# Weights converted 1024 columns at a time at fixed places in the program, and every engine's order fixed from the start

## The chip, the core and the metric

The kernel runs on one core of one Trainium2 chip. The time is the device time of one execution in microseconds (us). Before the change, three executions took 1067.61, 1067.10 and 1067.68 us, a median of 1067.61. The core has five engines that run side by side, each through its own queue of instructions in order: PE (matrix products; its weight loads are listed as PEld), DVE (vector), ACT (activation functions, scaled copies), POOL (elementwise work) and SP (starts DMA transfers). Results of PE land in PSUM, everything else is in SBUF.

## The reference

Eight batches of windowed attention (8 heads, 576 rows, head size 64, window 128, a linear bias per head) make a matrix x of 4608 rows by 512 columns. A two-layer network follows:

```python
attn = softmax(q @ k.T / 8 + bias, window of 128) @ v        # 8 batches x 8 heads x 576 x 64
x = attn laid out as (4608, 512)
h = x @ w_in                                                 # 512 -> 2048
g = h * tanh(log(1 + exp(h)))                                # mish
out = g @ w_out                                              # 2048 -> 512
```

q, k and v are 32-bit floats. [...]

## The kernel before

**Products.** Each 32-bit operand of the network is held as two parts, an upper part rounded to the format PE reads quickly, and the lower part that is left. A product is three matmuls: upper by upper, upper by lower, lower by upper.

**Weights.** There are 16 tiles, eight of `w_in` (raw `wi`, finished `si`) and eight of `w_out` (raw `wo`, finished `so`), called wi0 to wi7 and wo0 to wo7 here. A raw tile holds 1024 numbers of 64 bits per partition, read as pairs of 32-bit words (low, high). `convert_w` (lines 141 to 179) makes a 32-bit float of each and splits it, in two halves of 512 columns. For a half, ACT makes a scaled copy `t` (tile `ti` or `to`) and DVE shifts it by three bits and joins 29 bits of the low word into it. The sign then comes back in one of two ways: ACT takes the sign beforehand and POOL multiplies by it (`signs`), or DVE joins the sign bit with a third instruction. Last ACT writes the upper part and POOL subtracts it from the value, which gives the lower part.

**Chunks.** The 4608 rows go in nine chunks of 512. The first eight are rows 0 to 511 of each batch, the ninth collects the 64 left-over rows of all eight. `attention(b)` (line 401) makes chunk b's x in four pairs of heads, each of two units (`unit`: scores on PE, reduces and exps, a `fold` on POOL, a scale, transposes on PE, a mask on DVE, `values` on PE, `split_x`) and a small unit for the left-over rows. `first(c, j)` (line 433), j from 0 to 7, multiplies x by one `si` tile (24 matmuls into `h`) and ACT applies mish (`g`). `second(c, half, j, t)` (line 484) multiplies g by `so` tile j in 6 matmuls into `po`, in 32 steps: 16 for the first 256 rows, two for each j, then 16 for the rest. `parts` (line 452) splits g for it: ACT copies (`gh`), POOL subtracts (`gl`). The stages are attention(0), first of chunk 0, second of chunk 0 with attention(1) laid between its steps, first of chunk 1, and so on.

**Order.** SP's instructions keep the order in which they are written. Those of the other four engines are placed by a scheduler until the end of `first` of chunk 1, where `fixed` is set (line 534); from there they keep the written order too. `convert_next` (line 513) takes the next weight off a list: at three times inside attention(0) with both halves signed by ACT and POOL, in `first` of chunk 0 (none signed), and in `second` of chunk 0 (one half signed). The 16th weight, wo7, is loaded late into two smaller tiles, since space only then comes free.

Of the kernel before, what the change touches and what calls it, by code (L numbers as in the profile page):

```python
# [8 lines left out]
F32 = mybir.dt.float32  # L9
F32R = mybir.dt.float32r  # L10
U32 = mybir.dt.uint32
BF16 = mybir.dt.bfloat16
AF = mybir.ActivationFunctionType
ALU = mybir.AluOpType

WINDOW = 128
P = 128


class InOrder:  # L20


    def __init__(self, tc, engine, fixed):
        self.tc, self.engine, self.fixed = tc, engine, fixed

    def __getattr__(self, name):
        method = getattr(self.engine, name)

        def call(*args, **kwargs):
            ins = method(*args, **kwargs)  # L30
            if self.fixed:
                self.tc.keep_in_program_order(ins)
            elif name == "activation" and args[2] in (AF.Exp, AF.Mish, AF.Sign):

                self.tc.stamp_issue_order_token(ins.ins, "act_table")
            return ins

        return call

# [2 lines left out]
def attention_mish_mlp(  # L42
# [17 lines left out]
    nc = tc.nc  # L60
# [3 lines left out]
    CH = 512  # L64
# [26 lines left out]
    for t in vb:  # L91
# [5 lines left out]
    make_upper_triangular(nc, masks[:, 1, :])  # L97
    xs = dram.tile([NCC, P, CH], F32, tag="xs", name="xs")

    pe, dve, act, pool, sp = engines = [  # L100
        InOrder(tc, e, e in (nc.sync,))
        for e in (nc.tensor, nc.vector, nc.scalar, nc.gpsimd, nc.sync)
    ]

    bits = w_in.dtype != F32
    raw_w, split = {}, {}
# [32 lines left out]
    def convert_w(kind, j, signs):  # L141

        halves = raw_w.pop((kind, j))
        w = split[(kind, j)] = big(f"s{kind}{j}", F32R)
        for a, raw in enumerate(halves):
            if bits:
                low, high = raw[:, 0::2], raw[:, 1::2]  # L150
                val = high.bitcast(F32)
                t = ff.tile([P, 512], F32, tag="gh", name=f"t{kind}{j}_{a}", bufs=3)
                tb = t.bitcast(U32)

                act.activation(t, val, AF.Copy, scale=2.0**-112)
                if a < signs:
                    act.activation(val, val, AF.Sign)
                    out_ = tb
                else:
                    out_ = high  # L160
                dve.tensor_scalar(
                    out=out_, in0=tb, scalar1=3, scalar2=None, op0=ALU.logical_shift_left
                )
                dve.scalar_tensor_tensor(
                    out=out_, in0=low, scalar=29, in1=out_, op0=ALU.logical_shift_right,
                    op1=ALU.bitwise_or,
                )
                if a < signs:
# [6 lines left out]
            else:  # L175
                val = raw[:, :512].bitcast(F32)
            up, low = (w[:, 1024 * a + k : 1024 * a + k + 512] for k in (0, 512))
            act.activation(up, val, AF.Copy)
            pool.tensor_tensor(out=low, in0=val, in1=up.bitcast(F32), op=ALU.subtract)
# [10 lines left out]
    xt = {}  # L190
# [46 lines left out]
    def unit(b, p, half):  # L237
# [43 lines left out]
        def fold():  # L281
            sm, pz = st["sm"], st["pz"]
            two = pz if half else pz[:, 1:4:2]
            pool.tensor_tensor(out=two[:, :, :P], in0=two[:, :, :P], in1=two[:, :, P:], op=ALU.add)
            dve.tensor_scalar(out=sm, in0=sm, scalar1=1e-9, scalar2=None, op0=ALU.add)
            dve.reciprocal(sm, sm)

        def scale():
# [51 lines left out]
    def last_unit(b, p):  # L340
# [24 lines left out]

        def fold():
            sm, pz = st["sm"], st["pz"]
            dve.tensor_scalar(out=sm, in0=sm, scalar1=1e-9, scalar2=None, op0=ALU.add)
# [64 lines left out]
    def first(c, j):
        h = ps.tile([P, 2, CH], F32, tag="s", name=f"h{c}_{j}", bufs=2)
        for t in range(2):
            k = 0
            for cc in range(NCC):
                x = xt[(c, cc)]
                for w_, x_ in ((0, 0), (0, 1), (1, 0)):
                    k += 1  # L440
                    pe.matmul(
                        h[:, t, :], lhsT=w_part("i", j, w_, cc)[:, t * P : (t + 1) * P],
                        rhs=x[:, x_, :], start=(k == 1), stop=(k == 3 * NCC),
                    )
# [3 lines left out]
        act.activation(gt[(c, j // 2)][:, f : f + 2, :], h, AF.Mish)  # L448
# [61 lines left out]
    for w in conv[:-1]:  # L510
        load_w(*w)

    def convert_next(signs):
        if conv and conv[0] in raw_w:
            convert_w(*conv.pop(0), signs)

    early = [(k, lambda: convert_next(2)) for k in (3.6, 5.6, 7.6)]
    for _, work in sorted(attention(0) + early, key=lambda s: s[0]):
        work()

    for c in range(B + 1):
        for j in range(NJ):
            if c == 0:
                while ("i", j) not in split:
                    convert_next(0)
            if j == NJ - 1:
                parts(c, 0, 0)
                parts(c, 0, 1)
            first(c, j)
            if c == 0:  # L530
                convert_next(0)
# [84 lines left out]
```

## Time and profile before

| what | us |
|---|---|
| median of three executions | 1067.61 |
| the profiled execution | 1068.16 |
| its span, first instruction to last | 1066.4 |
| PE busy in the span | 1004.8 |
| first 90.9 us: PE busy | 44.83 of 84.20 |
| 133.9 to 218.6 (second of chunk 0): PE busy | 74.03 of 84.70 |

The profiled execution is 1.76 us longer than its span and 0.55 us longer than the median. All work records at line 30, where the helper `InOrder` issues it, so groups go by the names of tiles. In a row such as `so<-wo,so 128x512 fp32r<-128x512 f32 x2` the output stands left of the arrow, the inputs right of it, then shapes and types, and x2 says that two like instructions are drawn together. A bracket at a row's end is the idle time before it and the instruction that ended it. [...]

### The profile page before, as it was taken

How to read it: one execution, taken by the hardware profiler on the slowest of the kernel's cores; microseconds unless marked ns; L12 is line 12 of the kernel's file. 1: busy time of each engine (PE TensorE's matmuls, PEld its weight loads, DVE VectorE, ACT ScalarE, POOL GpSimd, SP SyncE). 2: the span in 40 equal slices, each digit the busy share in tenths (PEclk: the TensorE clock that was granted, in tenths of full speed). 3: DMA queues.
4: the chain of work that ended last, by engine and by line, in shares of the span. 5: the costliest groups of instructions: out<-in, count | busy, mean ns of one | idle time of the engine just before them, and what ended most of it. 6: DMA issues, size and time to landing. Idle time of an engine off the chain costs nothing.

```text
span 1066.4 us, 14184 instructions
## 1 busy us (share of the span) xinstructions
PE 1004.8 (94%) x5280; PEld 787.6 (74%) x5280; DVE 417.3 (39%) x1155; ACT 390.1 (37%) x937; POOL 324.0 (30%) x281
## 2 busy tenths in 40 slices
PE   4657987999999999999999999999999999999998
PEld 2335855788778877787778777877788778888886
DVE  3788189610671066305640375026601670010000
ACT  2445466422451254215431453244323442231121
POOL 3453667400431034104320343024301440151042
PEclk9568997999999999999999999999999999999999
DMA  8940021300221012200320031001200201010001
GB/s 272 399 150 11 1 65 37 90 33 1 60 84 41 1 51 67 67 1 26 92 67 1 25 92 58 10 24 59 72 31 1 61 33 41 1 41 20 1 1 40
DMA packets 52133, 59.32 MB, mean 56 GB/s; under 512 B 13024, under 2 KB 32608, under 8 KB 52064
## 3 DMA queue, kind: packets, MB, share of 16 engines
q1 hardware_dynamic: 50880, 57.69, 16.9%
q8 instruction: 42, 0.69, 0.3%
q10 hardware_dynamic: 1184, 0.72, 0.2%
q14 instruction: 27, 0.22, 0.1%
HBM read 47.91 MB, written 10.49 MB: 55 GB/s over the span
## 4 chain that ended last, share of the span: by engine, by line
PE 87%; DVE 6%; issue 3%; DMA 2%; ACT 1%; SPq 1%; POOL 0%; DVEq 0%; POOLq 0%
PE h L30 37%; PE po L30 36%; PE s L30 8%; PE o L30 5%; DVE pz L30 2%; DVE wo L30 1%; SPq L30 1%; DMA wi<-in_moe_w_in_dram 1%; DVE wi L30 1%; DVE sm L30 1%; DMA nb<-in_relb_dram 1%; DMA first<-in_k_dram 0%; DVE to L30 0%; DVE ti L30 0%; DMA qd<-in_q_dram 0%
## 5 line engine op out<-in xcount | busy, mean ns | idle before, releaser
L30 PE MATMUL h<-x,si 128*128 128x512 f32 x1728 | 396.5, 391 | 0.0
L30 POOL TENSOR_TENSOR gl<-g,gh 128x512 fp32r<-128x512 f32 x144 | 189.9, 1322 | 637.0 <-ACT gh L30 552.2
L30 PEld LDWEIGHTS h<-x,si 128*128 128x128 f32 x1728 | 326.0, 189 | 68.7 <-issue 0.8
L30 PE MATMUL po<-so,gh 128*128 128x512 f32 x1152 | 326.4, 403 | 2.8 <-POOL so L30 1.6
L30 PEld LDWEIGHTS po<-so,gh 128*128 128x128 f32 x1152 | 207.1, 189 | 53.4 <-ACT x L30 6.9
L30 DVE CUSTOM_DVE_ANT_0 pz<-s,nb 128x256 f32<-128x256 f32 (+1 forms) x256 | 84.5, 386 | 321.0 <-PE s L30 321.0
L30 PE MATMUL po<-so,gl 128*128 128x512 f32 x576 | 179.5, 393 | 0.0
L30 ACT ACTIVATE pz<-pz,mx 128x256 f32<-128x256 f32 (+1 forms) x256 | 120.3, 471 | 149.8 <-DVE mx L30 149.7
L30 ACT ACTIVATE g<-h 128x1024 f32<-128x1024 f32 x72 | 74.0, 1028 | 275.1 <-PE h L30 275.1
L30 PEld LDWEIGHTS po<-so,gl 128*128 128x128 f32 x576 | 108.4, 188 | 23.7
L30 ACT ACTIVATE gh<-g 128x512 fp32r<-128x512 f32 x144 | 88.4, 620 | 51.4 <-PE po L30 49.8
L30 DVE TENSOR_TENSOR pz<-s,masks 128x1024 f32<-128x1024 f32 x64 | 78.2, 1222 | 23.4 <-PE s L30 23.4
L30 POOL TENSOR_TENSOR pz<-pz 128x256 f32<-128x256 f32 x64 | 65.4, 1022 | 48.9 <-ACT pz L30 45.6
L30 DVE TENSOR_TENSOR pz<-pz,sm 128x512 f32<-128x512 f32 x56 | 53.8, 960 | 48.3 <-POOL pz L30 48.0
L30 DVE COPY ob<-po 128x512 f32<-128x512 f32 x18 | 12.4, 690 | 118.0 <-PE po L30 118.0
L30 PE MATMUL s<-qk 64*128 64x128 f32 (+1 forms) x448 | 58.4, 379 | 0.0
L30 PE MATMUL o<-pz,va 128*64 128x128 f32 (+1 forms) x560 | 56.4, 332 | 2.0 <-DVE pz L30 2.0
L30 PEld LDWEIGHTS o<-pz,va 128*64 128x64 f32 x560 | 34.1, 139 | 30.7 <-issue 12.3
L30 ACT ACTIVATE x<-o 128x512 fp32r<-128x512 f32 x32 | 19.1, 597 | 88.6 <-PE o L30 88.6
L30 PE MATMUL s<-ident,pz 128*128 128x128 f32 x256 | 41.4, 287 | 8.3 <-DVE pz L30 5.9
L30 ACT ACTIVATION_READ_ACCUMULATOR pz<-pz,mx 128x1 f32 x256 | 47.7, 186 | 0.0
L30 PEld LDWEIGHTS s<-ident,pz 128*128 128x128 f32 x256 | 33.0, 147 | 17.9 <-DVE pz L30 7.2
(122 smaller groups left out, 581.1 us busy)
## 6 DMA issues: line engine op xcount, KB each, us to landing
wi<-in_moe_w_in_dram SPq DMA_DIRECT2D x16, 512.0 KB, 10.4
wo<-in_moe_w_out_dram SPq DMA_DIRECT2D x16, 512.0 KB, 10.2
out_dram<-ob SPq DMA_DIRECT2D x32, 256.0 KB, 2.0
qk<-in_q_dram SPq DMA_DIRECT2D x28, 288.0 KB, 3.4
qk<-in_k_dram SPq DMA_DIRECT2D x28, 288.0 KB, 3.6
va<-in_v_dram SPq DMA_DIRECT2D x28, 256.0 KB, 2.9
first<-in_q_dram SPq DMA_DIRECT2D x4, 288.0 KB, 4.2
first<-in_k_dram SPq DMA_DIRECT2D x4, 288.0 KB, 4.8
```

The costliest lines, as they stand in the source:

```text
L30: ins = method(*args, **kwargs)
```

## The change

Conversion now works on the whole 1024 columns (only wo7, which lies in two tiles, keeps halves). `convert_w` returns four functions, and `converting` lays them at listed times into the steps of a stage. The instruction that shifted a single input by a constant (TENSOR_SCALAR) becomes one with a second input, a column of zeros that is broadcast (SCALAR_TENSOR_TENSOR). The same is done to the small `sm + 1e-9`.

```diff
-    pe, dve, act, pool, sp = engines = [
-        InOrder(tc, e, e in (nc.sync,))
+    pe, dve, act, pool, sp = (
+        InOrder(tc, e) for e in (nc.tensor, nc.vector, nc.scalar, nc.gpsimd, nc.sync)
+    )
+    zero = const.tile([P, 1], U32, tag="zero", name="zero")
...
+        n = 512 if (kind, j) == last_w else 1024
+        parts_ = halves if n == 512 else [whole[(kind, j)]]
...
+            st["t"] = t = ff.tile([P, 1024], F32, tag="gg", name=f"t{kind}{j}", bufs=3)
...
-                dve.tensor_scalar(
-                    out=out_, in0=tb, scalar1=3, scalar2=None, op0=ALU.logical_shift_left
+                dve.scalar_tensor_tensor(
+                    out=out_, in0=tb, scalar=3, in1=zero.to_broadcast([P, n]), op0=ALU.logical_shift_left,
+                    op1=ALU.bitwise_or,
                 )
...
+        return scaled, joined, upper, lower
...
-        gh = ff.tile([P, 2, 256], F32R, tag="gh", name=f"gh{c}_{half}_{j}", bufs=3)
-        gl = ff.tile([P, 2, 256], F32R, tag="gl", name=f"gl{c}_{half}_{j}", bufs=3)
+        gg = ff.tile([P, 2, 2, 256], F32R, tag="gg", name=f"gg{c}_{half}_{j}", bufs=3)
+        gh, gl = gg[:, 0], gg[:, 1]
...
-    early = [(k, lambda: convert_next(2)) for k in (3.6, 5.6, 7.6)]
+    early = attention(0) + converting(
+        conv[:3], [(4.3, 4.8, 5.6, 5.7), (5.5, 6.35, 7.1, 7.2), (7.0, 8.1, 8.7, 8.8)], True
+    )
+    early += [
+        (8.6, lambda: first(0, 0, (0,))),
+        (9.03, lambda: first(0, 0, (1, 2))),
+        (9.04, lambda: first(0, 0, (3,))),
+    ]
...
+            starts = [-0.5 + 0.78 * n for n in range(10)]
+            steps += converting(
+                conv[3:13], [(t, t + 0.3, t + 1.1, t + 1.15) for t in starts], False
+            )
...
+            steps += converting(
+                conv[13:], [(0.5, 1.5, 3.5, 3.6), (2.5, 3.6, 5.5, 5.6), (6.0, 7.0, 9.0, 9.1)], True
+            )
```

So three weights (wi0 to wi2, signed) are converted in attention(0), ten (wi3 to wo4, unsigned) in `first` of chunk 0, and three (wo5 to wo7, signed) in `second` of chunk 0. `first` is split from its mish, which is issued at time j + 0.9 of the phase. The merged tile `gg` holds both parts of g, and the scaled copies `ti` and `to` take turns in its three buffers.

Three places in the order of instructions follow. First DVE at the end of attention(0); `x_3` is the last piece of chunk 0's x, `pz_3_1` the last unit's weights, and the `wi` and `ti` rows are conversions. Before:

```order
L30 COPY xo_3l<-pt_3l 128x64
L30 SCALAR_TENSOR_TENSOR wi_149<-ti_1_669,wi_149 128x512
L30 RECIPROCAL sm_3_1_519<-sm_3_1_519 128x4
L30 TENSOR_SCALAR wi_152<-ti_0_704 128x512
L30 SCALAR_TENSOR_TENSOR wi_152<-wi_152 128x512
L30 TENSOR_SCALAR wi_152<-ti_1_711 128x512
L30 SCALAR_TENSOR_TENSOR wi_152<-ti_0_704,wi_152 128x512
L30 SCALAR_TENSOR_TENSOR wi_152<-wi_152 128x512
L30 TENSOR_SCALAR wi_155<-ti_0_745 128x512
L30 SCALAR_TENSOR_TENSOR wi_152<-ti_1_711,wi_152 128x512
L30 TENSOR_SCALAR wi_155<-ti_1_752 128x512
L30 SCALAR_TENSOR_TENSOR wi_155<-wi_155 128x512
```

And now:

```order
L30 RECIPROCAL sm_3_1_507<-sm_3_1_507 128x4
L30 COPY xo_3l<-pt_3l 128x64
L30 SCALAR_TENSOR_TENSOR ti_497<-ti_497,zero 128x1024
L30 SCALAR_TENSOR_TENSOR ti_497<-wi_145,ti_497 128x1024
L30 TENSOR_TENSOR pz_3_1_508<-s_3_1_491,masks 128x2x4x128
L30 TENSOR_TENSOR x_3_575<-o_3_537,x_3_575 128x512
L30 SCALAR_TENSOR_TENSOR wi_148<-ti_597,zero 128x1024
L30 SCALAR_TENSOR_TENSOR wi_148<-wi_148 128x1024
L30 SCALAR_TENSOR_TENSOR wi_148<-ti_597,wi_148 128x1024
L30 SCALAR_TENSOR_TENSOR wi_151<-ti_603,zero 128x1024
```

Before, conversions of four later weights stood ahead of the last mask; now two instructions of wi2 stand there, and wi3 (`wi_148`) begins behind `x_3`.

Second, ACT in `first` of chunk 0; `g` from `h_j` is the mish of phase j, `si` and `so` are upper parts. Before:

```order
L30 ACTIVATE g_1_701<-h_2_676 128x1024
L30 ACTIVATE si_703<-wi_152 128x512 x2
L30 ACTIVATE si_744<-wi_155 128x512 x2
L30 ACTIVATE gh_0_2_951<-g_1_701 128x512
L30 ACTIVATE g_1_701<-h_3_718 128x1024
L30 ACTIVATE g_2_784<-h_4_759 128x1024
L30 ACTIVATE si_786<-wi_158 128x512 x2
L30 ACTIVATE so_827<-wo_161 128x512 x2
L30 ACTIVATE g_2_784<-h_5_801 128x1024
L30 ACTIVATE g_3_867<-h_6_842 128x1024
```

And now:

```order
L30 ACTIVATE si_679<-wi_160 128x2x512
L30 ACTIVATE g_1_682<-h_3_689 128x1024
L30 ACTIVATE to_749<-wo_166 128x1024
L30 ACTIVATE so_714<-wo_163 128x2x512
L30 ACTIVATE g_2_756<-h_4_723 128x1024
L30 ACTIVATE to_759<-wo_169 128x1024
L30 ACTIVATE so_748<-wo_166 128x2x512
L30 ACTIVATE to_792<-wo_172 128x1024
L30 ACTIVATE g_2_756<-h_5_761 128x1024
L30 ACTIVATE so_758<-wo_169 128x2x512
L30 ACTIVATE to_826<-wo_175 128x1024
```

The mish of phase 3 now stands behind the upper part of wi7 (`wi_160`), that of phase 4 behind wo0's, that of phase 5 behind wo1's.

Third, DVE in `second` of chunk 0, around the first unit of pair 1 of attention(1), written `1_0`; ISA rows with `nb` are its reduces, and `wo_176`, `wo_179`, `to_1012` are weights. Before:

```order
L30 TENSOR_SCALAR wo_176<-to_1_1083 128x512
L30 ISA pz_1_0_1147,mx_1_0_1145<-s_1_0_1122,nb 128x128
L30 ISA mx_1_0_1145 128x1
L30 ISA pz_1_0_1147,mx_1_0_1145<-s_1_0_1122,nb 128x128
L30 ISA mx_1_0_1145 128x1
L30 ISA pz_1_0_1147,mx_1_0_1145<-s_1_0_1122,nb 128x256
L30 ISA mx_1_0_1145 128x1
L30 ISA pz_1_0_1147,mx_1_0_1145<-s_1_0_1122,nb 128x256
L30 ISA mx_1_0_1145 128x1
L30 ISA pz_1l,mx_1l<-s_1_0_1122,nl 128x192
L30 ISA mx_1l 128x1
L30 SCALAR_TENSOR_TENSOR wo_176<-wo_176 128x512
```

And now:

```order
L30 ISA pz_1_0_1039,mx_1_0_1037<-s_1_0_1030,nb 128x128
L30 ISA mx_1_0_1037 128x1
L30 SCALAR_TENSOR_TENSOR to_1012<-to_1012,zero 128x512
L30 SCALAR_TENSOR_TENSOR to_1012<-wo_0_869,to_1012 128x512
L30 SCALAR_TENSOR_TENSOR to_1012<-to_1012,zero 128x512
L30 SCALAR_TENSOR_TENSOR to_1012<-wo_1_870,to_1012 128x512
L30 ISA pz_1_0_1039,mx_1_0_1037<-s_1_0_1030,nb 128x256
L30 ISA mx_1_0_1037 128x1
L30 ISA pz_1_0_1039,mx_1_0_1037<-s_1_0_1030,nb 128x256
L30 ISA mx_1_0_1037 128x1
L30 TENSOR_TENSOR pz_0_1_954<-s_0_1_947,masks 128x2x4x128
```

All four join instructions of wo7 now stand between the reduces of that unit and ahead of the mask of the unit before it.

## Rows read from the trace of the kernel before

**Rows 1.** The page: span, busy time by engine, and the share of each engine in the chain that ended last.

```profile
span 1066.4 us, 14184 instructions
...
PE 1004.8 (94%) x5280; PEld 787.6 (74%) x5280; DVE 417.3 (39%) x1155; ACT 390.1 (37%) x937; POOL 324.0 (30%) x281
...
PE 87%; DVE 6%; issue 3%; DMA 2%; ACT 1%; SPq 1%; POOL 0%; DVEq 0%; POOLq 0%
```

**Rows 2.** Busy time by stage: stretch, its length, busy us (and instructions) of PE, PEld, DVE, ACT and POOL, granted PE clock, DMA share, GB/s. The last row is a whole later chunk.

```profile
6.70:90.90 84.20, 44.83 (x238) 29.32 (x238) 63.27 (x160) 35.54 (x102) 34.11 (x28) 0.67 0.69 246
90.90:133.90 43.00, 43.00 (x187) 35.24 (x185) 16.36 (x25) 23.66 (x35) 23.23 (x18) 0.97 0.00 0
133.90:218.60 84.70, 74.03 (x409) 53.05 (x409) 69.32 (x158) 43.89 (x117) 50.62 (x38) 0.92 0.20 61
182.20:218.60 36.40, 36.13 (x216) 27.42 (x215) 25.12 (x71) 15.10 (x48) 16.16 (x13) 1.00 0.23 68
331.10:442.30 111.20, 111.20 (x613) 87.55 (x612) 43.59 (x134) 40.47 (x104) 28.51 (x24) 1.00 0.15 45
```

**Rows 3.** PE in order of time (start, length): in attention(0) the first scores of pairs 1 to 3 (`s<-first`), transposes of pair 2's second unit (59.54) and of the last unit (81.35), and the last values (88.99); then the start of `second` of chunk 0, its longest wait (174.38) and, by count of `po` matmuls, its 15th step (j = 7) at 182.18; last the whole first phase of a later chunk.

```profile
20.02 2.45 PE L30 MATMUL s<-first 64*128 64x128 f32 x12
...
38.25 2.75 PE L30 MATMUL s<-first 64*128 64x128 f32 x12
...
55.80 2.46 PE L30 MATMUL s<-first 64*128 64x128 f32 x12
59.54 1.11 PE L30 MATMUL s<-ident,pz 128*128 128x128 f32 x4 [1.27 <-POOL pz L30]
...
81.35 0.66 PE L30 MATMUL s<-ident,pz 128*128 128x128 f32 x4 [0.52 <-POOL pz L30]
88.99 1.97 PE L30 MATMUL o<-pz,first 128*64 128x128 f32 x12 [6.98 <-DVE pz L30]
...
135.21 1.17 PE L30 MATMUL po<-so,gh 128*128 128x512 f32 x4
...
174.38 1.12 PE L30 MATMUL s<-ident,pz 128*128 128x128 f32 x4 [4.94 <-DVE pz L30]
...
182.18 1.31 PE L30 MATMUL po<-so,gh 128*128 128x512 f32 x4
...
331.10 43.68 PE L30 MATMUL h<-x,si 128*128 128x512 f32 x192
```

**Rows 4.** DVE in attention(0), in order of time: the last instruction of the first weights ahead of pair 1's reduces, and the first of those reduces; then the last mask.

```profile
26.48 0.69 DVE L30 SCALAR_TENSOR_TENSOR ti<-wi,ti 128x512 uint32<-128x512 uint32 x1
27.09 0.28 DVE L30 CUSTOM_DVE_ANT_0 pz<-s,nb 128x128 f32<-128x128 f32 x1
...
87.72 1.21 DVE L30 TENSOR_TENSOR pz<-s,masks 128x1024 f32<-128x1024 f32 x1
```

**Rows 5.** DVE while POOL had nothing to do.

```profile
94.72 0.42 DVE L30 TENSOR_SCALAR wo<-to 128x512 uint32<-128x512 uint32 x1
95.06 0.68 DVE L30 SCALAR_TENSOR_TENSOR wi<-ti,wi 128x512 uint32<-128x512 uint32 x1
95.66 0.68 DVE L30 SCALAR_TENSOR_TENSOR wo<-to,wo 128x512 uint32<-128x512 uint32 x1
```

**Rows 6.** DVE, then POOL, in one stretch in which both had work.

```profile
104.42 1.49 DVE L30 TENSOR_SCALAR wo<-to 128x512 uint32<-128x512 uint32 x1 [3.79 <-ACT to L30]
105.95 1.66 DVE L30 SCALAR_TENSOR_TENSOR wo<-wo 128x512 uint32<-128x512 uint32 x1
107.64 1.67 DVE L30 SCALAR_TENSOR_TENSOR wo<-to,wo 128x512 uint32<-128x512 uint32 x1
...
100.11 5.52 POOL L30 TENSOR_TENSOR si<-wi,si 128x512 fp32r<-128x512 f32 x4 [15.67 <-ACT si L30]
105.59 3.17 POOL L30 TENSOR_TENSOR gl<-g,gh 128x512 fp32r<-128x512 f32 x2
```

**Rows 7.** POOL in order of time: two subtractions with no conversion on DVE beside them, the last lower part of a weight (wo7), and a fold of 128x256 and one of 128x512 elements.

```profile
121.93 2.59 POOL L30 TENSOR_TENSOR so<-wo,so 128x512 fp32r<-128x512 f32 x2
...
176.97 1.28 POOL L30 TENSOR_TENSOR pz<-pz 128x512 f32<-128x512 f32 x1
...
182.78 1.31 POOL L30 TENSOR_TENSOR so<-wo,so 128x512 fp32r<-128x512 f32 x1 [1.39 <-ACT so L30]
...
186.53 0.73 POOL L30 TENSOR_TENSOR pz<-pz 128x256 f32<-128x256 f32 x1
```

**Rows 8.** POOL, then DVE, grouped, from 133.6 to 184.1 (count, busy us, mean ns, idle before and what ended it).

```profile
L30 POOL TENSOR_TENSOR so<-wo,so 128x512 fp32r<-128x512 f32 x12 | 17.1, 1431 | 5.3 <-ACT so L30 5.2
L30 POOL TENSOR_TENSOR gl<-g,gh 128x512 fp32r<-128x512 f32 x6 | 9.1, 1521 | 0.6 <-ACT gh L30 0.6
L30 POOL TENSOR_TENSOR wo<-to,wo 128x512 f32<-128x512 f32 x5 | 6.7, 1339 | 9.3 <-ACT pz L30 5.0 <-PE pt_1l L30 3.0 <-PE s L30 0.7
...
L30 DVE SCALAR_TENSOR_TENSOR wo<-wo 128x512 uint32<-128x512 uint32 x5 | 5.4, 1082 | 0.1
L30 DVE SCALAR_TENSOR_TENSOR to<-wo,to 128x512 uint32<-128x512 uint32 x5 | 5.4, 1079 | 0.1
...
```

**Rows 9.** ACT: the copy of x, and two upper parts of 512 columns.

```profile
91.01 0.60 ACT L30 ACTIVATE x<-o 128x512 fp32r<-128x512 f32 x1 [3.38 <-PE o L30]
...
99.36 1.26 ACT L30 ACTIVATE si<-wi 128x512 fp32r<-128x512 f32 x2
```

More of the change, by code (lines that the diff above doesn't have):

```diff
@@ L20, with __init__ @@
 class InOrder:
-    def __init__(self, tc, engine, fixed):
-        self.tc, self.engine, self.fixed = tc, engine, fixed
+    def __init__(self, tc, engine):
+        self.tc, self.engine = tc, engine
     def __getattr__(self, name):
@@ L29, in call @@
         def call(*args, **kwargs):
[L30 to L36, printed above, removed]
+            return self.tc.keep_in_program_order(method(*args, **kwargs))
         return call
@@ L98, in attention_mish_mlp @@
     xs = dram.tile([NCC, P, CH], F32, tag="xs", name="xs")
-    pe, dve, act, pool, sp = engines = [
-        InOrder(tc, e, e in (nc.sync,))
-        for e in (nc.tensor, nc.vector, nc.scalar, nc.gpsimd, nc.sync)
-    ]
+    pe, dve, act, pool, sp = (
+        InOrder(tc, e) for e in (nc.tensor, nc.vector, nc.scalar, nc.gpsimd, nc.sync)
+    )
+    zero = const.tile([P, 1], U32, tag="zero", name="zero")
+    pool.memset(zero, 0)
     bits = w_in.dtype != F32
-    raw_w, split = {}, {}
+    raw_w, whole, split = {}, {}, {}
     last_w = ("o", NJ - 1)
@@ L132, in load_w @@
             halves = [t[:, :1024], t[:, 1024:]]
+            whole[(kind, j)] = t
         raw_w[(kind, j)] = halves
@@ L139, in load_w, with convert_w, scaled, joined @@
                 load(t[:, :512].bitcast(F32).rearrange("p (c n) -> p c n", n=n), part)
-    def convert_w(kind, j, signs):
+    def convert_w(kind, j, sign):
         halves = raw_w.pop((kind, j))
-        w = split[(kind, j)] = big(f"s{kind}{j}", F32R)
-        for a, raw in enumerate(halves):
-            if bits:
+        n = 512 if (kind, j) == last_w else 1024
+        parts_ = halves if n == 512 else [whole[(kind, j)]]
+        st = {}
+        def scaled():
+            st["w"] = split[(kind, j)] = big(f"s{kind}{j}", F32R)
+            if not bits:
+                return
+            st["t"] = t = ff.tile([P, 1024], F32, tag="gg", name=f"t{kind}{j}", bufs=3)
+            for a, raw in enumerate(parts_):
+                val = raw[:, 1::2].bitcast(F32)
+                act.activation(t[:, a * n : (a + 1) * n], val, AF.Copy, scale=2.0**-112)
+                if sign:
+                    act.activation(val, val, AF.Sign)
+        def joined():
+            if not bits:
+                return
+            for a, raw in enumerate(parts_):
                 low, high = raw[:, 0::2], raw[:, 1::2]
-                val = high.bitcast(F32)
-                t = ff.tile([P, 512], F32, tag="gh", name=f"t{kind}{j}_{a}", bufs=3)
+                t = st["t"][:, a * n : (a + 1) * n]
                 tb = t.bitcast(U32)
[L155 to L160, printed above, removed]
-                dve.tensor_scalar(
-                    out=out_, in0=tb, scalar1=3, scalar2=None, op0=ALU.logical_shift_left
+                out_ = tb if sign else high
+                dve.scalar_tensor_tensor(
+                    out=out_, in0=tb, scalar=3, in1=zero.to_broadcast([P, n]), op0=ALU.logical_shift_left,
+                    op1=ALU.bitwise_or,
                 )
@@ L167, in convert_w @@
                 )
-                if a < signs:
+                if sign:
+                    val = high.bitcast(F32)
                     pool.tensor_tensor(out=val, in0=t, in1=val, op=ALU.mult)
@@ L174, in convert_w, with values_and_places, upper, lower @@
                     )
[L175 to L179, printed above, removed]
+        def values_and_places():
+            w = st["w"].rearrange("p (a u n) -> p a u n", a=2, u=2)
+            if bits and n == 1024:
+                val = parts_[0][:, 1::2].bitcast(F32).rearrange("p (a n) -> p a n", a=2)
+                yield val, w[:, :, 0, :], w[:, :, 1, :]
+                return
+            for a, raw in enumerate(halves):
+                val = raw[:, 1::2].bitcast(F32) if bits else raw[:, :512].bitcast(F32)
+                yield val, w[:, a, 0, :], w[:, a, 1, :]
+        def upper():
+            for val, up, _ in values_and_places():
+                act.activation(up, val, AF.Copy)
+        def lower():
+            for val, up, low in values_and_places():
+                pool.tensor_tensor(out=low, in0=val, in1=up.bitcast(F32), op=ALU.subtract)
+        return scaled, joined, upper, lower
     def w_part(kind, j, part, c):
@@ L284, in fold @@
             pool.tensor_tensor(out=two[:, :, :P], in0=two[:, :, :P], in1=two[:, :, P:], op=ALU.add)
-            dve.tensor_scalar(out=sm, in0=sm, scalar1=1e-9, scalar2=None, op0=ALU.add)
+            dve.scalar_tensor_tensor(
+                out=sm, in0=sm, scalar=1e-9, in1=sm, op0=ALU.add, op1=ALU.max
+            )
             dve.reciprocal(sm, sm)
@@ L367, in fold @@
             sm, pz = st["sm"], st["pz"]
-            dve.tensor_scalar(out=sm, in0=sm, scalar1=1e-9, scalar2=None, op0=ALU.add)
+            dve.scalar_tensor_tensor(
+                out=sm, in0=sm, scalar=1e-9, in1=sm, op0=ALU.add, op1=ALU.max
+            )
             dve.reciprocal(sm, sm)
@@ L431, in attention_mish_mlp, with first, mish @@
     gt = {}
[L433 to L444, printed above, removed]
+    def first(c, j, blocks=range(NCC)):
+        if blocks[0] == 0:
+            hs[j % 2] = ps.tile([P, 2, CH], F32, tag="s", name=f"h{c}_{j}", bufs=2)
+        h = hs[j % 2]
+        for t, cc in (
+            [(t, cc) for cc in blocks for t in range(2)] if len(blocks) < NCC
+            else [(t, cc) for t in range(2) for cc in blocks]
+        ):
+            x = xt[(c, cc)]
+            for k, (w_, x_) in enumerate(((0, 0), (0, 1), (1, 0))):
+                pe.matmul(
+                    h[:, t, :], lhsT=w_part("i", j, w_, cc)[:, t * P : (t + 1) * P],
+                    rhs=x[:, x_, :], start=(cc == 0 and k == 0), stop=(cc == NCC - 1 and k == 2),
+                )
+    hs = {}
+    def mish(c, j):
         if j % 2 == 0:
@@ L447, in first @@
         f = 2 * (j % 2)
[L448 removed]
+        act.activation(gt[(c, j // 2)][:, f : f + 2, :], hs[j % 2], AF.Mish)
     gs = {}
@@ L511, in attention_mish_mlp, with run, converting @@
         load_w(*w)
-    def convert_next(signs):
-        if conv and conv[0] in raw_w:
-            convert_w(*conv.pop(0), signs)
-    early = [(k, lambda: convert_next(2)) for k in (3.6, 5.6, 7.6)]
-    for _, work in sorted(attention(0) + early, key=lambda s: s[0]):
-        work()
+    def run(steps):
+        for _, work in sorted(steps, key=lambda s: s[0]):
+            work()
+    def converting(weights, times, sign):
+        steps = []
+        for (kind, j), at_ in zip(weights, times):
+            st = []
+            steps.append((at_[0], lambda kind=kind, j=j, st=st: st.extend(convert_w(kind, j, sign))))
+            steps += [(t, lambda n=n, st=st: st[n]()) for n, t in enumerate(at_)]
+        return steps
+    early = attention(0) + converting(
+        conv[:3], [(4.3, 4.8, 5.6, 5.7), (5.5, 6.35, 7.1, 7.2), (7.0, 8.1, 8.7, 8.8)], True
+    )
+    early += [
[3 more added lines that the diff above has]
+    ]
+    run(early)
     for c in range(B + 1):
+        steps = []
         for j in range(NJ):
[L523 to L531, printed above, removed]
+            if c or j:
+                steps.append((j, lambda j=j: first(c, j)))
+            steps.append((j + 0.9, lambda j=j: mish(c, j)))
+        steps += [(NJ - 1.05, lambda j=j: parts(c, 0, j)) for j in range(2)]
+        if c == 0:
+            starts = [-0.5 + 0.78 * n for n in range(10)]
+            steps += converting(
+                conv[3:13], [(t, t + 0.3, t + 1.1, t + 1.15) for t in starts], False
+            )
+        run(steps)
         if c == 0:
             load_w(*last_w)
-        if c == 1:
-            for e in engines:
-                e.fixed = True
         n = 4 * NJ
@@ L544, in attention_mish_mlp @@
                 steps.append((2 * m - 4.1, lambda m=m: parts(c, *divmod(m, NJ))))
-            if c == 0:
-                steps.append((2 * m + 0.5, lambda: convert_next(1)))
+        if c == 0:
+            steps += converting(
+                conv[13:], [(0.5, 1.5, 3.5, 3.6), (2.5, 3.6, 5.5, 5.6), (6.0, 7.0, 9.0, 9.1)], True
+            )
         if c + 1 < B:
@@ L550, in attention_mish_mlp @@
             steps.append((4.5, last_x))
-        for _, work in sorted(steps, key=lambda s: s[0]):
-            work()
+        run(steps)
 _INS = ["q", "k", "v", "moe_w_in", "moe_w_out"]
```

## The prediction

> **What bounds the kernel now.** I read busy times and the chain that ended last first. PE is busy for 1004.8 of 1066.4 us and holds 87% of that chain [rows 1]. The stages come next: a later chunk keeps PE busy for all of its 111.20 us at a granted clock of 1.00, so nothing that this change touches can shorten it. PE waits in two places only: in attention(0), 39.4 of 84.20 us, and in the second phase of chunk 0, 10.7 of 84.70 us at a clock of 0.92 [rows 2]. Everything to gain or lose lies ahead of 218.6 us.
>
> What do the waits come from? In PE's order the long ones end at DVE: 6.98 us before the last values of attention(0), and 4.94 us at 174.38 [rows 3]. DVE is late there because it converts weights, and it converts slowly because of POOL. With POOL idle the instructions of a half follow each other after 0.34 us (shift), 0.60 and 0.60 [rows 5]. With POOL at work the same ones take 1.49, 1.66 and 1.67 us, and POOL's pair of `gl` takes 3.17 instead of 2.59 [rows 6, 7]. The starts fit strict turns: one POOL instruction of 1.28, one DVE instruction of 0.6, and so on. So a DVE instruction with its inputs in SBUF and a POOL instruction share one way, whatever the DVE form. The quantity to add up is the work on this shared way.
>
> From 133.6 to 184.1, when wo7's last lower part ends [rows 7], it held: 12 lower parts, 5 `gl`, 5 multiplications at 1.28 (the sixth `gl` begins behind it), four folds (2 x 1.28 + 2 x 0.73), five shifts for each of the two kinds of half at 0.34, 15 joins at 0.60, and about 2.6 (an estimate) of scales and small instructions [rows 5, 7, 8]. That is 28.2 + 4.0 + 3.4 + 9.0 + 2.6 = 47.2 of 50.5 us, or 93%. PE's step with j = 7 began at 182.18 and needs that lower part; from there PE is busy for 36.13 of 36.40 us at full clock [rows 2, 3]. The shared way sets the end of chunk 0.
>
> **The change, part by part.**
>
> *End of attention(0).* Pair 1's first scores are written by 20.02 + 2.45 = 22.47, but its reduces start at 27.09 behind weights that were still arriving [rows 3, 4]: 4.6 us. The change converts nothing before pair 2, so the 18.23 from 20.02 to 38.25 becomes 13.6. The next pair takes 17.55 as before (38.25 to 55.80), since its first weights come in it now, and I allow the same for the last pair's first part: 20.0 + 13.6 + 17.55 + 17.55 = 68.7. The last unit's transposes follow 3.74 + 1.11 later (59.54 against 55.80), at 73.6. Before the change the mask then came at 87.72, 5.7 us after the transposes' end at 82.0, behind conversions of later weights; now wi2's two joins stand there, 1.2 to 2.3 us, then 1.21 of mask and 1.97 of values. With 0.6 for the copy of x and 1.0 for wi3's scaled copy [rows 9] the first unsigned conversion begins at about 79.6 (78.4 if the joins are done early, 83 if they also wait for a 1024-wide POOL instruction). The first phase's matmuls run from a little ahead of that, 78, where 90.9 stood [rows 2].
>
> *Ten weights in the first phase.* The list lays them 0.78 of a phase apart, and a phase lasts 43.68/8 = 5.46 [rows 3], so it asks for one per 4.26 us. (The second phase of a chunk is then 111.20 - 43.68 = 67.5.) Three 1024-wide DVE instructions: 0.60 is 0.53 of columns and 0.07 fixed, so 1.14 each. The new shift with a second input goes at this rate, not at the 0.34 per half of the old: 3.42 for a weight against 3.08, so 0.34 lost for each. POOL's subtraction of 1024 lies between 2.38 and 2.56 (twice 1.28, with or without a saved start); I take 2.40. On the shared way a weight costs 5.82, and the ten take 58.2, to 137.8. The pace of the list isn't met. PE waits for that: the mish of phases 3 to 7 stand behind the upper parts of later weights on ACT, with every upper part behind DVE. From the list, phase 7's products can end only shortly ahead of 134, and the second phase begins at about 135 against 135.21 [rows 3]. The 13 us gained in attention(0) are spent waiting for conversions; what they buy is that two more weights are finished by then.
>
> *Second phase of chunk 0.* Left on the shared way up to `gl` 7: wo5 and wo6, each 2 x 1.14 + 2 x 2.40 = 7.1; wo7 in halves, 4 x 0.60 + 4 x 1.28 = 7.5; eight `gl`, 10.2; folds 2 x 0.73 + 1.28 = 2.7; scales and small ones 2.6. Sum 37.2, and at the 93% of before 40.0. It ends at 137.8 + 40.0 = 177.8, where 184.1 stood. The step with j = 7 needs `gl` 7 about 0.9 us after its start; I leave this aside for small waits and let it start at 178.0, where 182.18 stood: 4.2 us earlier. Its remaining 36.4 us have no wait to lose.
>
> *The rest.* The tiny `sm` instruction keeps its place; its result is needed only behind the fold, whose 0.73 to 1.28 us on POOL hide it [rows 7], and without that cover the difference of two forms on four columns is no more than the 0.07 fixed cost. The merged `gg` has three buffers for what had three each; scaled copies took `gh`'s before, so cover is as good. Later chunks were in written order already: nothing, since PE never waits there.
>
> [...]
>
> Sum: 1068.16 - 4.2 = 1063.96 for an execution like the profiled one. That one lay 0.55 above the median, so the median should be **1063.4**. The ends: start 78.4 to 83 (-1.2 to +3.4); 1024-wide subtractions at 2.38 to 2.56 (14 of them: -0.3 to +2.2); the shared way filled to 100% or only 86% (-2.8 to +3.3). Together about 1058 to 1070.
>
> **Rivals.** *B: wide instructions don't take turns.* If a second input that is broadcast, or the wide form, left POOL its way, DVE's 3.42 would hide beside POOL's 2.40 and the list's 4.26 would hold. The first phase would end near 78 + 44 = 122 and the second near 122 + 67.5 + 2 = 191 against 218.6: about 1040. [...] Against it: three different forms waited for POOL [rows 6]. Half of the effect would give 1052.
>
> *C: slower, by wo7's joins.* They stand in DVE's order between the reduces of pair 1's first unit and ahead of the previous unit's mask. Each may wait for a POOL instruction, 1.28 to 2.40 us, together 5 to 9.6. Queued behind them are the reduces, so ACT's exps, POOL's fold, DVE's scale and PE's transposes and values. The sum counts the joins' own place on the shared way, but not that the way runs empty while that chain catches up. PE's clock makes it worse: before, 84.7 x (1 - 0.92) = 6.8 us went to the clock beside 10.7 of idle time [rows 2], 0.64 for each. So 5 to 9.6 becomes 8 to 16, less 4.2: slower by 4 to 12, about 1074. It decides from 2.6 us of such waiting on (2.6 x 1.64 = 4.2). For it: the 4.94 us wait was of this kind. Against it: before, DVE had 25 conversion instructions among the same reduces and masks.
>
> That the change doesn't do what it says can't be: the new order stands in the program.
>
> **Chances.** A, the sum: 0.60. C: 0.27. B, whole or half: 0.13. A measurement tells about 0.2% (2.1 us) from no change. Within A, 1063.4 lies 4.2 under the median of before: faster by over 0.2% 0.37, within 0.13, slower 0.10. C gives slower 0.23, within 0.04. B gives faster 0.13. Together: faster 0.50, same 0.17, slower 0.33. The range 1051 to 1076 holds A, half of B and most of C; A's own is 1058 to 1070.
>
> **What would show it.** First `h` matmuls running without a break from about 78; `si` and `so` lower parts on POOL 5.8 us apart up to 138, with DVE's joins at 1.1 alone and over 3 beside a POOL instruction; PE waits of some 13 us in the first phase that end at ACT or POOL; the second phase's start near 135 and its 15th step near 178; later chunks at 111.2. Lower parts 4.3 us apart would mean B. Waits of PE on the masks and scales of pairs 0 and 1, longer than 4.94 together by 2.6 or more, would mean C. A start of phase 0 later than 83 would break the first term.

## The result and the profile after

The changed kernel takes 1074.26 us (median of four executions, 1072.83 to 1076.08) against 1067.64: a ratio of 1.0063 with a 95% interval of 1.0046 to 1.0081. It is slower by 6.6 us, where 4.2 us less were forecast. The profiled execution took 1073.70 us, its span 1072.0, which is 5.6 more than before.

The page of the kernel after, where [rows 1] stood for before:

```profile
span 1072.0 us, 14004 instructions
...
PE 1007.2 (94%) x5280; PEld 792.4 (74%) x5280; DVE 433.4 (40%) x1114; ACT 389.1 (36%) x903; POOL 325.1 (30%) x263
...
PE 85%; DVE 7%; issue 4%; POOL 2%; ACT 1%; DMA 1%; POOLq 0%; ACTq 0%; DVEq 0%
```

The chain gives two hundredths less of itself to PE, and more to DVE, POOL and issue. The stages of the kernel after, with the columns of [rows 2] (granted clock: PE's clock as the profile records it, as a share of full speed). The first row ends at 80.00, ahead of the last unit's work (the 4.95 us up to 84.95 aren't shown); the later rows begin with PE's long run of `h` matmuls, with the second phase, with its 14th step and with the next chunk:

```profile
6.70:80.00 73.30, 40.39 (x213) 27.21 (x213) 49.02 (x128) 27.76 (x83) 26.69 (x20) 0.94 0.80 282
...
84.95:139.17 54.22, 45.69 (x189) 36.63 (x187) 52.47 (x30) 29.29 (x29) 30.15 (x10) 0.93 0.06 19
139.17:184.99 45.82, 33.75 (x161) 24.76 (x162) 35.81 (x70) 27.19 (x61) 33.79 (x21) 0.85 0.12 36
184.99:225.66 40.67, 40.67 (x262) 30.98 (x260) 25.28 (x74) 15.59 (x49) 16.07 (x14) 1.00 0.23 68
225.66:336.00 110.34, 110.34 (x610) 86.84 (x609) 43.34 (x134) 40.80 (x104) 28.48 (x24) 1.00 0.14 44
```

From 181.61 on PE never waits in chunk 0: the whole loss lies ahead of it. PE in order of time (start, length, wait), to hold against [rows 3]:

```profile
18.63 2.75 PE L30 MATMUL s<-first 64*128 64x128 f32 x12
...
32.40 2.75 PE L30 MATMUL s<-first 64*128 64x128 f32 x12
...
49.68 2.75 PE L30 MATMUL s<-first 64*128 64x128 f32 x12
...
64.08 1.98 PE L30 MATMUL o<-pz,first 128*64 128x128 f32 x12 [8.52 <-DVE pz L30]
...
84.95 26.38 PE L30 MATMUL h<-x,si 128*128 128x512 f32 x114
116.09 19.31 PE L30 MATMUL h<-x,si 128*128 128x512 f32 x72 [4.77 <-ACT g L30]
139.17 1.65 PE L30 MATMUL s<-qk 64*128 64x128 f32 x8 [3.77 <-ACT g L30]
...
156.55 1.12 PE L30 MATMUL s<-ident,pz 128*128 128x128 f32 x4 [4.27 <-DVE pz L30]
...
169.79 1.09 PE L30 MATMUL s<-ident,pz 128*128 128x128 f32 x4 [4.34 <-DVE xo_0l L30]
...
188.80 1.63 PE L30 MATMUL po<-so,gg 128*128 128x512 f32 x6
```

Pair 1 of attention(0) is short, as expected: the scores of pair 2 start at 32.40 instead of 38.25, those of pair 3 at 49.68 instead of 55.80. It is 6 us ahead there and still only 6 us ahead where the first phase's run of matmuls begins (84.95 against 90.9), although later weights no longer stand in front of the last mask: something in between took back what that should have given. The 15th step (j = 7) begins at 188.80, where 182.18 stood. What happens at 49.68 shows in DVE's own order of the kernel after:

```profile
49.14 0.18 DVE L30 RECIPROCAL sm<-sm 128x4 f32<-128x4 f32 x1
61.56 0.22 DVE L30 COPY xo_2l<-pt_2l 128x64 f32<-128x64 f32 x1 [12.24 <-DMA xs<-xo_0l]
61.70 0.28 DVE L30 CUSTOM_DVE_ANT_0 pz<-s,nb 128x128 f32<-128x128 f32 x1
```

DVE stands still for 12.24 us with a copy of 0.22 at the head of its queue. `xo` (the left-over rows' results) has two buffers, so the third pair's copy needs the first pair's store to have landed. Pair 3's reduces, whose scores PE had written at 52.4, queue behind it. The store itself, in SP's order (start, issue time) and in the list of transfers of that stretch (KB each, median us from issue to landing), kernel after:

```profile
49.79 1.60 SPq L30 DMA_DIRECT2D wo<-in_moe_w_out_dram  x2
52.39 0.33 SPq L30 DMA_DIRECT2D xs<-xo_0l  x1
53.67 0.33 SPq L30 DMA_DIRECT2D xs<-xo_1l  x1
```

```profile
xs<-xo_0l SPq DMA_DIRECT2D x1, 32.0 KB, 9.1
```

SP issues 30 loads of weights first, and the store then lands 9.1 us after its issue: 52.39 + 9.1 = 61.5. In the kernel before the store was as late (issued at 51.91, 9.1 us to landing), but its scheduler had put the copy behind pair 3's reduces and other conversions, where no wait was left. DVE of the kernel before:

```profile
66.67 0.21 DVE L30 COPY xo_2l<-pt_2l 128x64 f32<-128x64 f32 x1
```

From 86.74 on the conversions run at the pace that the sum had. DVE, then POOL of the kernel after, one weight and the next:

```profile
102.31 1.21 DVE L30 SCALAR_TENSOR_TENSOR wi<-ti,zero 128x1024 uint32<-128x1024 uint32 x1
103.56 1.23 DVE L30 SCALAR_TENSOR_TENSOR wi<-wi 128x1024 uint32<-128x1024 uint32 x1
104.81 3.35 DVE L30 SCALAR_TENSOR_TENSOR wi<-ti,wi 128x1024 uint32<-128x1024 uint32 x1
108.08 1.22 DVE L30 SCALAR_TENSOR_TENSOR wi<-ti,zero 128x1024 uint32<-128x1024 uint32 x1
```

```profile
97.93 3.36 POOL L30 TENSOR_TENSOR si<-wi,si 128x1024 fp32r<-128x1024 f32 x1 [2.42 <-ACT si L30]
103.65 3.43 POOL L30 TENSOR_TENSOR si<-wi,si 128x1024 fp32r<-128x1024 f32 x1 [2.35 <-ACT si L30]
109.50 3.33 POOL L30 TENSOR_TENSOR si<-wi,si 128x1024 fp32r<-128x1024 f32 x1 [2.42 <-ACT si L30]
```

DVE's third instruction takes 3.35 us, since POOL's 2.4 falls into it (the lower part at 74.32, with no conversion on DVE beside it, took 2.41); POOL's takes 3.4, since a DVE instruction falls into it. A weight takes 5.77 us (102.31 to 108.08).

### The profile page after: what moved, and what is told of

It reads as the page before. It is cut to its first block, busy times and chain, and to the rows that moved or that the text cites. A ratio compares the mean times of both kernels' runs of the same rounds, so it can differ in the third digit from the quotient of the medians.

```text
span 1072.0 us, 14004 instructions
## 1 busy us (share of the span) xinstructions
PE 1007.2 (94%) x5280; PEld 792.4 (74%) x5280; DVE 433.4 (40%) x1114; ACT 389.1 (36%) x903; POOL 325.1 (30%) x263
## 4 chain that ended last, share of the span: by engine, by line
PE 85%; DVE 7%; issue 4%; POOL 2%; ACT 1%; DMA 1%; POOLq 0%; ACTq 0%; DVEq 0%
PE po L30 37%; PE h L30 33%; PE s L30 9%; PE o L30 5%; DVE wo L30 2%; DVE wi L30 2%; DVE pz L30 1%; DVE to L30 1%; POOL pz L30 1%; DMA nb<-in_relb_dram 1%; ACT pz L30 1%; POOL so L30 0%; DVE pz_2l L30 0%; POOL gg L30 0%; DMA first<-in_k_dram 0%
## 5 line engine op out<-in xcount | busy, mean ns | idle before, releaser
L30 PE MATMUL po<-so,gg 128*128 128x512 f32 x1728 | 433.1, 401 | 0.2 <-POOL gg L30 0.2
L30 POOL TENSOR_TENSOR gg<-g,gg 128x512 fp32r<-128x512 f32 x144 | 188.6, 1313 | 652.3 <-ACT gg L30 584.9
L30 PEld LDWEIGHTS po<-so,gg 128*128 128x128 f32 x1728 | 317.2, 190 | 74.1 <-ACT x L30 6.6
L30 ACT ACTIVATE gg<-g 128x512 fp32r<-128x512 f32 x144 | 88.5, 621 | 46.6 <-PE po L30 46.6
L30 PEld LDWEIGHTS s<-qk 64*128 64x128 f32 x448 | 34.4, 188 | 15.0 <-issue 8.2
L30 DVE SCALAR_TENSOR_TENSOR sm<-sm 128x4 f32<-128x4 f32 x64 | 36.3, 568 | 12.5 <-ACT pz L30 12.5
```

The lines of the kernel that those rows point to most:

```text
L30: return self.tc.keep_in_program_order(method(*args, **kwargs))
```

## The experiments

Each was timed in alternation with the kernel before, whose median was 1066.5 to 1067.2 there. "After" means 1074.3; its four executions spread over 3.3 us, so a difference of 2 us from it tells little.

**Four buffers for `xo`.**

```diff
-            xo = at.tile([P, LEFT], F32, tag="xo", name=f"xo{name}")
+            xo = at.tile([P, LEFT], F32, tag="xo", name=f"xo{name}", bufs=4)
```

> The changed kernel with four buffers for xo instead of two, nothing else. Theory 1 (the 12.24 us in which DVE's copy of xo_2l waits for the store of xo_0l stand in front of everything): the wait goes, wi3's first join starts near 86.7 - 12.2 = 74.5, the second phase near 139.2 - 12.2 = 127, later stages keep their lengths, and the time is 1074.3 - 12 = about 1062 (1060 to 1064). Rival (the time is set further on, by the order in the second phase or by weights that are still arriving): the 12 us come back as waits before 186 us, and the time stays within 3 us of 1074.

Measured: 1065.19 us, 0.9983 of before (0.9973 to 0.9992). DVE, two lines of this kernel:

```profile
47.07 0.23 DVE L30 COPY xo_2l<-pt_2l 128x64 f32<-128x64 f32 x1 [0.48 <-PE pt_2l L30]
...
77.45 1.23 DVE L30 SCALAR_TENSOR_TENSOR wi<-ti,zero 128x1024 uint32<-128x1024 uint32 x1 [0.35 <-ACT ti L30]
```

The copy no longer waits for a store, the unsigned conversions start at 77.45 instead of 86.74, and the time falls by 9.1 of the 12.24 us (pair 3 then waits for PE and POOL instead: from the copy to the first unsigned conversion it is 30.38 us, where 25.18 stood). With two buffers the copy came at 61.56 in the kernel after, and at 60.56 and 61.41 in the next two experiments, however early DVE was ready for it (waits of 12.24, 14.78 and 13.91 us). This one wait costs more than the whole loss: without it the change is faster than before, by 0.17%.

**The one-input shift again, 1024 wide.**

```diff
-                dve.scalar_tensor_tensor(
-                    out=out_, in0=tb, scalar=3, in1=zero.to_broadcast([P, n]), op0=ALU.logical_shift_left,
-                    op1=ALU.bitwise_or,
-                )
+                dve.tensor_scalar(
+                    out=out_, in0=tb, scalar1=3, scalar2=None, op0=ALU.logical_shift_left
+                )
```

> The changed kernel with the shift as TENSOR_SCALAR with one input again, in the new 1024 columns. Theory 2 (the way that DVE and POOL share is full from 86.7 to 181, so its work is what counts): a 1024-wide shift takes about 0.61 instead of 1.14 us, ten weights 5.3 us less, wo5 to wo7 1.5 less: lower parts 5.25 us apart instead of 5.77 and a time of 1074.3 - 6.5 = about 1068. Rival (what counts is the order of the attention's steps, or the one-input form waits for POOL longer): no more than 2 us either way.

Measured: 1065.88, 8.4 less than after, and 0.9994 of before (0.9984 to 1.0003), no different from it. Two lower parts in a row on POOL:

```profile
105.36 2.82 POOL L30 TENSOR_TENSOR si<-wi,si 128x1024 fp32r<-128x1024 f32 x1 [2.43 <-ACT si L30]
110.64 2.80 POOL L30 TENSOR_TENSOR si<-wi,si 128x1024 fp32r<-128x1024 f32 x1 [2.45 <-ACT si L30]
```

They stand 5.28 us apart, as theory 2 had it; the time fell by 1.9 us more than it said. The shift with a second, broadcast input costs 0.5 us a weight and gives nothing back.

**A slower pace in the first phase.**

```diff
-            starts = [-0.5 + 0.78 * n for n in range(10)]
+            starts = [-0.5 + 1.06 * n for n in range(10)]
```

> The changed kernel with the ten weights laid 1.06 of a phase apart instead of 0.78, so that a phase's mish no longer stands behind uppers that are late. Theory 2 (the shared way's total work sets the end of chunk 0): PE's two waits for ACT (4.77 and 3.77 us) go and the second phase starts near 130 instead of 139, but its steps wait longer, and the time stays within 2.5 us of 1074. Rival (the order of ACT is what costs: the waits were lost time): 8.5 us less, about 1066.

Measured: 1076.03, 1.8 more than after, not told apart from it. PE of this kernel:

```profile
84.89 42.45 PE L30 MATMUL h<-x,si 128*128 128x512 f32 x186
...
149.99 2.93 PE L30 MATMUL po<-so,gg 128*128 128x512 f32 x6 [14.18 <-ACT gg L30]
...
191.13 1.63 PE L30 MATMUL po<-so,gg 128*128 128x512 f32 x6
```

The first phase now runs without one wait, and its whole gain of over 10 us is paid back in one wait of 14.18. Where PE waits can be chosen; when chunk 0 ends hardly changes (15th step at 191.13, after 188.80). The rival (ACT's order) falls.

**wo6 and wo7 behind the attention's steps.**

```diff
-                conv[13:], [(0.5, 1.5, 3.5, 3.6), (2.5, 3.6, 5.5, 5.6), (6.0, 7.0, 9.0, 9.1)], True
+                conv[13:], [(0.5, 1.5, 3.5, 3.6), (4.5, 6.35, 7.2, 7.25), (6.6, 7.6, 9.6, 9.7)], True
```

> The changed kernel with wo6's joins laid behind pair 0's last scale, and wo7's behind the mask, in the second phase of chunk 0; the same work. Theory 3 (attention's steps queue behind conversions, as rival C had it): PE's waits of 4.34 us (at 169.8) and 1.55 us (at 176.2) go or shrink, the time falls by 4 to 8 to about 1068. Theory 2 (the shared way is full until 181): the same work takes as long, within 2 us of 1074.

Measured: 1075.82, 1.5 more than after, not told apart from it. PE of this kernel:

```profile
182.38 1.09 PE L30 MATMUL s<-ident,pz 128*128 128x128 f32 x4 [8.94 <-DVE pz L30]
```

The waits of 4.34 and 1.55 are gone and one of 8.94 stands a little later. Theory 3, which was rival C, gets no support: with these joins in another order the kernel takes as long. Other orders weren't run.

**Both gains together** (four buffers and the one-input shift).

> Four buffers for xo and the one-input shift together. Theories 1 and 2 (two separate losses: an idle stretch before 74, and work on the shared way after it): the gains add, 1074.3 - 9.1 - 8.4 = about 1057, faster than both kernels. Rival (both remove the same wait, or the second hides behind the first): no better than 1062.

Measured: 1057.13, 0.9907 of before (0.9892 to 0.9921). The gains add to within 0.4 us: two separate losses, one in front of the other. (This kernel is called e5 below.)

**Lower parts on DVE.**

```diff
-                pool.tensor_tensor(out=low, in0=val, in1=up.bitcast(F32), op=ALU.subtract)
+                (pool if sign else dve).tensor_tensor(
+                    out=low, in0=val, in1=up.bitcast(F32), op=ALU.subtract
+                )
```

> The changed kernel with the lower parts of the ten unsigned weights subtracted by DVE instead of POOL. Theory 2 (DVE and POOL take strict turns, so only the sum of their lengths counts): 2.40 us of POOL become 1.25 of DVE, a weight takes four times 1.25 = 5.0 instead of 5.77 us, the ten 7.7 us less, time about 1066.5. Rival (DVE is the bound by itself, with the shift's extra work, and POOL worked beside it): the fourth instruction on DVE makes it slower, 1076 or more.

Measured: 1066.36, 7.9 less than after; 0.9995 of before (0.9986 to 1.0005). DVE of this kernel, one weight:

```profile
95.11 1.22 DVE L30 SCALAR_TENSOR_TENSOR wi<-ti,zero 128x1024 uint32<-128x1024 uint32 x1
96.36 1.23 DVE L30 SCALAR_TENSOR_TENSOR wi<-wi 128x1024 uint32<-128x1024 uint32 x1
97.62 1.23 DVE L30 SCALAR_TENSOR_TENSOR wi<-ti,wi 128x1024 uint32<-128x1024 uint32 x1
98.76 1.22 DVE L30 TENSOR_TENSOR si<-wi,si 128x1024 fp32r<-128x1024 f32 x1
99.90 1.22 DVE L30 SCALAR_TENSOR_TENSOR wi<-ti,zero 128x1024 uint32<-128x1024 uint32 x1
```

Putting all the work on one engine, with the other idle, is quicker than sharing it: four instructions in 4.79 us against 5.77. That fits a POOL instruction that stops DVE's for nearly its whole length: the third instruction takes 1.23 us alone and 3.35 with POOL's 2.4 inside. It doesn't fit to the last tenth: DVE's three take 3.65 us here without POOL (95.11 to 98.76), and with POOL's 2.40 that would be 6.05, where the kernel after takes 5.77. About 0.3 us a weight does overlap. Masks, which read the scores from PSUM, weren't stopped: in the kernel after, the one at 81.20 took 1.22 us wholly beside a POOL instruction (81.09 to 83.50), and the one at 72.99, with none beside it, 1.22 too.

**Halves again, at the same places.**

```diff
-        n = 512 if (kind, j) == last_w else 1024
-        parts_ = halves if n == 512 else [whole[(kind, j)]]
+        n = 512
+        parts_ = halves
```

> The changed kernel with all conversions in halves of 512 columns again, at the same places. Theory 2: six DVE instructions at 0.63 and two subtractions at 1.28 make 6.3 us a weight instead of 5.77, ten weights 5.5 us more: about 1080. Rival (the wide form costs, since each wait for the other engine is 2.4 us long): 1072 or less.

Measured: 1079.49, 5.2 more than after; 1.0116 of before (1.0101 to 1.0131). The 1024-wide form is a gain by itself, with three instructions on DVE and one on POOL a weight instead of six and two.

**All three** (e8_all below): four buffers, the one-input shift, and lower parts of the ten weights on DVE.

> Four buffers for xo, the one-input shift, and lower parts of the ten unsigned weights on DVE. Theory 2: a weight takes 0.72 + 3 x 1.25 = 4.5 us on the way, under a phase's 5.46, so PE should run through the first phase with hardly a wait; 1057 - 7.7 = about 1049 if all of it arrives. Rival (PE's own work in the first phase bounds from there on): half of that gain, 1053.

Measured: 1051.37, 0.9851 of before (0.9837 to 0.9866): faster than both kernels by 1.5% and more. PE of this kernel:

```profile
72.99 42.48 PE L30 MATMUL h<-x,si 128*128 128x512 f32 x186
...
132.38 1.11 PE L30 MATMUL s<-ident,pz 128*128 128x128 f32 x4 [6.24 <-DVE pz L30]
145.35 1.09 PE L30 MATMUL s<-ident,pz 128*128 128x128 f32 x4 [3.29 <-DVE xo_0l L30]
```

The first phase has no wait. 5.8 of the expected 7.7 us arrived; the wait for pair 0's first scale in the second phase grew (6.24, where e5 had 4.62).

**wo5 to wo7 on DVE too** (e9_second below), unsigned (the kernel above, with `False` for `True` in the second list).

> The kernel of e8_all with wo5 to wo7 converted without ACT's sign and POOL's multiplication, and their lower parts on DVE too. Theory 2: a weight's 0.72 + 1.25 + 2 x 2.40 = 6.8 us on the shared way become 0.72 + 3 x 1.25 = 4.5, three weights 6.9 us less where the way is still full: about 1051.4 - 6 = 1045. Rival (in the second phase the chain of attention's steps is the bound by now, and more work stands ahead of its steps on DVE): 1051 or slower.

Measured: 1052.07, no gain. PE of this kernel, its long waits in the second phase:

```profile
133.59 1.12 PE L30 MATMUL s<-ident,pz 128*128 128x128 f32 x4 [5.39 <-DVE pz L30]
...
143.23 1.54 PE L30 MATMUL o<-pz,va 128*64 128x256 f32 x8 [4.13 <-DVE pz L30]
...
155.80 1.97 PE L30 MATMUL o<-pz,va 128*64 128x128 f32 x12 [3.13 <-DVE pz L30]
```

Theory 2 has reached its end here: with less work on the shared way, what PE waits for is the attention's own masks and scales, queued behind conversions on DVE (the mask that ends the 4.13 ran from 141.97, two reduces behind a conversion that had begun at 139.19).

**Lower parts of g in the first half of chunk 0 on DVE** (on top of the last).

```diff
-        pool.tensor_tensor(out=gl, in0=src, in1=gh.bitcast(F32), op=ALU.subtract)
+        (dve if c == 0 and half == 0 else pool).tensor_tensor(out=gl, in0=src, in1=gh.bitcast(F32), op=ALU.subtract)
```

> The kernel of e9_second with the eight lower parts of g of chunk 0's first half on DVE as well (0.65 instead of 1.28 us each, 5 us less on the way). Theory 2: 3 to 5 us less than e9_second. Rival (DVE's queue, which now holds everything, delays the attention's steps): the same as e9_second or slower.

Measured: 1050.49, 0.9852 of before (0.9836 to 0.9868). This is 1.6 less than the last, where theory 2 had 3 to 5, and 0.9 less than the kernel with all three, whose executions spread over 2.5 us: not told apart from it.

## Why the prediction was wrong

**What failed: the end of attention(0).** The sum had the first unsigned conversion at 79.6, 83 at the latest; it came at 86.74. Pair 1's 13.6 measured 13.8 (18.63 to 32.40), and the next pair's 17.55 measured 17.3. The step "I allow the same for the last pair's first part" is the one that broke. By it the last unit's transposes begin 21.3 us (17.55 + 3.74) after pair 3's first scores; they began 30.3 us after them (49.68 to 79.98), and 23.2 us with four buffers. The sign that the prediction named for this, a first phase later than 83, appeared (84.95). The step counted DVE's work there, but not the copy of `xo_2l` that program order puts ahead of pair 3's reduces, nor the store that this copy waits for. Without that wait the start is 77.45, 2.2 us earlier than forecast, and the time 1065.2 where 1063.4 stood. The sign of the forecast hangs on this one omitted wait.

**What held: the pace of the shared way.** Ten weights were put at 58.2 us (5.82 each); they run at 5.77. Part of this fit is luck. DVE's three instructions were put at 3.42 from rows of instructions that don't read what the one before them wrote; they take 3.65, and the 0.3 us that overlaps with POOL makes up for it. The split behind the 3.42, 0.53 us for 512 columns and 0.07 fixed, stands in no row, but measured steps bear it out: with lower parts on DVE the join at 97.62, 1.23 us long for 1024 columns (1.20 ns a column), makes way after 1.14, and one of 512 columns after 0.60 [rows 5]. The two forms of the small `sm` instruction took 0.158 us before and 0.153 after, at their shortest. Three runs that changed only the work on the way moved the time by 8.4, 7.9 and 5.2 us, with 6.5, 7.7 and 5.5 expected.

**What also failed: PE's step with j = 7.** From 86.74, the forecast's 58.2 and 40.0 end at 184.9, and `gl` 7 ended at 185.4. That is luck too: POOL ended wo7's lower parts at 180.91 and then waited 3.22 us for ACT's copy, while the sum had put its idle time, 7%, on the way itself. And the step doesn't hang on `gl` 7, as the prediction has it. PE's last wait ended at 181.61, with a scale on DVE that stood in its queue behind wo7's joins and ran beside POOL's lower parts of wo7 (1.80 us; the next one, at 188.18, took 0.69). PE, DVE and POOL of the kernel after:

```profile
181.61 0.64 PE L30 MATMUL s<-ident,pz 128*128 128x128 f32 x4 [1.63 <-DVE pz L30]
...
179.66 1.80 DVE L30 TENSOR_TENSOR pz<-pz,sm 128x512 f32<-128x512 f32 x1
...
178.35 2.56 POOL L30 TENSOR_TENSOR so<-wo,so 128x512 fp32r<-128x512 f32 x2
184.13 1.30 POOL L30 TENSOR_TENSOR gg<-g,gg 128x512 fp32r<-128x512 f32 x1 [3.22 <-ACT gg L30]
```

From there PE has 7.2 us of its own work up to the 15th step, without a wait: 181.61 to 188.80. The same 7.2 stand in the runs with four buffers (171.95 to 179.14), the one-input shift (173.04 to 180.22) and the slower pace (183.92 to 191.13). In the kernel before, PE's wait for the same scale ended at 174.38, and the step began 7.8 us later [rows 3]. So the end of chunk 0 is reached through this scale; that the work on the shared way decides when it runs fits the three runs above, but wasn't shown by itself.

In numbers: start 7.1 too late, the step another 3.7 (178.0 + 7.1 is 185.1, against 188.80), later stages 1.0 better. That makes 9.8, the difference between a span 4.2 shorter and one 5.6 longer. A's range has a slip besides: its ends add up to 1059.1 and 1072.3, not to 1058 and 1070; 1074.3 lies above both.

**The first phase.** The mish of phases 3 and 6 did wait for later weights' uppers (wi7's and wo3's), but PE's two waits were 8.5 us and not some 13. Another 2.7 us went into matmuls that ran slower behind the first wait (72 in 19.31 us, against 114 in 26.38), at a granted clock of 0.85 against 1.00.

**Rivals.** C gave 1074 and a slower kernel, which is what was measured, but by luck: what costs most is the wait for the store. Its sign did appear: PE's waits on the scales and masks of pairs 0 and 1 add up to 11.8 us (4.27, 4.34, 1.55 and 1.63), 6.9 more than the 4.94 it was to be held against. But the kernel before had more such waits than that one, 7.9 us in all, so the sign was set too low. And wo7's joins, which C blames, took 4.2 us (170.1 to 174.3), PE lost 1.55 behind them, and moving them gained nothing. B falls: lower parts stand 5.77 apart, not 4.3, and the wide form and the broadcast input take turns with POOL like the others.

## What to carry to other kernels

When a scheduler's order is replaced by a written one, go through every instruction that reuses a small buffer and ask what the last reader is waiting for: here a 32 KB store behind 15 MB of loads stopped an engine for 12 us, and with two more buffers of 256 bytes a partition the kernel took 9.1 us less. Where two engines take turns on one path, add up their work as if they were one engine, and give each piece to the engine that does it in less time, even if the other then idles. In a stage that such a sum bounds, moving two of the waits gained nothing here; taking work out did, until the next chain showed.

## What the runs showed of the hardware

That DVE and POOL in turns would let a sum of lengths predict three whole runs to 2 us was more than expected (the one for wo5 to wo7 missed by 7), and so was that one engine alone beats the pair (4.79 against 5.77 us a weight). A small store took 9.1 us from issue to landing behind the loads, and 1.6 (`xo_2l`) once they were through. With lower parts on DVE, an instruction that reads what the one before it wrote started 1.25 us after it at 1024 columns (95.11 to 96.36), one that doesn't 1.14 (97.62 to 98.76): about 0.1 us for the dependence.
